# Retention plus gated layer on one core: three operand sums of the first seven-product tile moved together on VectorE, the others halved on GpSimd

## The chip, the cores and the metric

The kernel runs on one core of one Trainium2 chip. The time is device microseconds for one execution of the whole program; less is better. It is given as the median of five runs. A profile of one further execution shows where its time went. "n" counts token tiles, "x" the products of one tile, as in the code.

## The reference

Eight batches of 576 tokens, eight heads of 64: a retention layer (scores of q and k, times a decay per head and distance, lower triangle only, times v), whose output, laid out as 4608 tokens by 512, goes through a layer of width 2048:

```python
scores = scale * np.matmul(q, k.transpose(0, 1, 3, 2))
Dmat = np.where(rel >= 0, gamma[:, None, None] ** rel[None, :, :], 0.0)
x = np.matmul(scores * Dmat, v)        # to [4608, 512]
h = x @ w_in                           # [4608, 2048]
out = (h * np.cos(h)) @ w_out          # [4608, 512]
```

## The kernel before

**Groups and tiles.** Tokens are handled in 36 groups g of 128 for the retention part and in ten tiles n for the layer, of 512 tokens except n = 1 and 2 (256 each). Tile 3 (S7 in the code) is the first, and tile 9 the last, that uses the scheme described below. Everything is issued in an order written out by hand; each engine runs its own queue in that order, and waits are put in where data or buffers demand it.

**The retention part of a group.** `load` brings q, k and v from memory on SyncE's queue. `prep` scales q and k by the decays and casts v (L139, L140, L147, mostly on GpSimd). `transposes` turns the scaled q and k by a DMA transpose (L156). `scores` (L183) multiplies them into the two-bank tiles "a" and "b"; VectorE applies the mask (L192, tile `ret`). `states` (L242) makes the running state of a pair of groups in bank "b"; VectorE copies or adds it out (L263, L265), and ScalarE spreads it into blocks (L256). `attn_out` (L283, L296) uses state and `ret`, and ScalarE writes the result as x (L308). In tile 3, `unit7` does this for groups 12 to 15 between the products, in the order states, attention output, scores of the next pair. The second `scores` of a pair uses bank "b" and so must wait until L263 and L265 have read the states there.

**The layer.** `mm1` makes a block of h in PSUM (L323), ScalarE the cosine (L331), VectorE the product gT (L332). Tile 3 has eight such blocks i = 0 to 7.

**Seven products in place of eight.** From tile 3 on, gT and w_out are taken as two by two quarters, and the second matrix product is made by seven quarter products instead of eight (`mm2_seven`, `product`, L457). Their order is x = 3, 4, 5, 2, 1, 7, 6. Products 5, 2, 1, 7 and 6 need sums or differences of two quarters of gT first, which `g_sum` makes (L398). Its arguments are the tile, the product, and a range of the eight row blocks: 0 to 4 and 4 to 8 are the two halves, 0 to 8 is a whole sum. A half is a 128x1024 instruction, a whole 128x2048.

`g_sum` chooses the engine. In tile 3 products 5 and 1 and the second half of 6 are on VectorE, the rest on GpSimd; in the last tile 5 and 1 are on VectorE; in the others only 5. Behind each sum of product 5 a gate is set: the next sum that goes to GpSimd is made to wait for it ("port free" in the code). `sums_after` calls `g_sum` after the blocks of `mm1`; in tile 3, two more calls stand inside `mm2_seven`: whole sum 1 on VectorE ahead of the addition to u22, and the second half of 6 on VectorE ahead of the store of c12.

**The outputs of a tile.** Four quarters of the output are gathered in SBUF: c12, c21, u11 and u22. ScalarE copies, and VectorE adds or subtracts product after product (`add`, L477). Products 5, 2 and 6 accumulate onto PSUM tiles of earlier products, so they can begin only when these have been read: product 2 onto product 4's tile, which the first addition to u22 reads. Each `store` puts a DMA on SyncE's queue and calls `feed`, which issues the next preps on GpSimd, and transposes and loads on SyncE. In tile 3 `prep_next` handles group 16 between the sums on GpSimd; groups 17 to 21 follow from the stores.

Of the kernel before, what the change touches and what calls it, by code (L numbers as in the profile page):

```python
# [17 lines left out]
def kernel(  # L18
# [34 lines left out]
    widths = [512, 256, 256] + [512] * 7  # L53
# [3 lines left out]
    S7 = 3  # L57
# [42 lines left out]
    tiles = {}  # L100
# [253 lines left out]
    E2 = ET // 2  # L354
    N2 = DM // 2
    w_sum = {}

    def w_quarter(r, c):
        return w_out_sb[:, r * E2 : (r + 1) * E2, c * N2 : (c + 1) * N2]

    def w_sums(x, e0, e1):

        a, b, op_ = {
            3: ((0, 1), (1, 1), ALU.subtract),
            4: ((1, 0), (0, 0), ALU.subtract),
            1: ((0, 0), (1, 1), ALU.add),
            6: ((0, 0), (0, 1), ALU.add),
            7: ((1, 0), (1, 1), ALU.add),
        }[x]
        if x in (3, 4):  # L370
            w_sum[x] = w_quarter(*a)
        elif x not in w_sum:
            pool, tag = {1: (consts, "ws1"), 6: (first, "qs4"), 7: (first, "qT4")}[x]
            w_sum[x] = pool.tile([P, E2, N2], BF16, tag=tag, name=f"ws{x}")
        nc.vector.tensor_tensor(
            out=w_sum[x][:, e0:e1],
            in0=w_quarter(*a)[:, e0:e1],
            in1=w_quarter(*b)[:, e0:e1],
            op=op_,
        )  # L380

    def g_sum(n, x, e0, e1):

        gT = tiles["g", n]
        a, b, op_ = {
            5: ((0, 0), (0, 1), ALU.add),
            2: ((1, 0), (1, 1), ALU.add),
            1: ((0, 0), (1, 1), ALU.add),
            7: ((0, 1), (1, 1), ALU.subtract),
            6: ((1, 0), (0, 0), ALU.subtract),  # L390
        }[x]
        if ("gs", n, x) not in tiles:
            tiles["gs", n, x] = sump.tile([P, E2, 256], BF16, tag=f"gs{x}", name=f"gs{x}")
        i0, i1 = (
            gT[:, k * E2 + e0 : k * E2 + e1, r * 256 : (r + 1) * 256] for r, k in (a, b)
        )
        on_dve = {S7: x in (5, 1) or (x, e0) == (6, 4), len(widths) - 1: x in (5, 1)}.get(n, x == 5)
        i = (nc.vector if on_dve else nc.gpsimd).tensor_tensor(  # L398
            out=tiles["gs", n, x][:, e0:e1], in0=i0, in1=i1, op=op_
        )  # L400
        if x == 5:
            tiles["gate"] = i
        elif "gate" in tiles and not on_dve:
            tc.add_manual_dep(
                i.ins,
                tiles.pop("gate").ins.name,
                mybir.DependencyInfo(mybir.DependencyClass.Sync, mybir.DependencyReason.DATA),
                reason="port free",
            )

    def sums_after(n, i):

        if n == S7:
            if i < 4:
                w_sums(3 + i % 2, i // 2 * 4, i // 2 * 4 + 4)
            if i == 6:
                g_sum(n, 5, 0, 4)
                g_sum(n, 2, 0, 4)
            elif i == 7:
                g_sum(n, 5, 4, E2)  # L420
                g_sum(n, 2, 4, E2)
                g_sum(n, 7, 0, E2)
                prep_next()
                g_sum(n, 6, 0, 4)
        elif i in (3, 7):
            for x in (5, 2, 1, 7, 6):
                g_sum(n, x, i - 3, i + 1)

    last = len(widths) - 1

    def product(n, x):

# [34 lines left out]
    def mm2_seven(n, at):  # L467

        s0 = starts[n] // P
        pend = []  # L470

        def flush():
            while pend:
                pend.pop(0)()

        def add(out_, in0, in1, op_=ALU.add):
            pend.append(lambda: nc.vector.tensor_tensor(out=out_, in0=in0, in1=in1, op=op_))  # L477

        def new(tag):
            return op.tile([P, 2, N2], F32, tag=tag, name="ot")  # L480

        def store(t, r, c, s):
            r0 = starts[n] + r * 256
            nc.sync.dma_start(
                out[r0 : r0 + 256, c * N2 : (c + 1) * N2].rearrange("(j p) c -> p j c", p=P), t
            )
            feed(s)

        for x in (3, 4, 5, 2, 1, 7, 6):
            if x in at:  # L490
                at[x](flush)
            else:
                flush()
            parts = product(n, x)
            if x == 3:
                u22 = new("a")
                nc.scalar.copy(u22, tiles["all", 3])
            elif x == 4:
                if n == S7:
                    g_sum(n, 1, 0, E2)  # L500
                add(u22, tiles["all", 4], u22)
            elif x == 5:
                c12, u11 = new("c"), new("b")
                nc.scalar.copy(c12, tiles["all", 3])
                add(u11, u22, tiles["all", 3], ALU.subtract)
                if n == S7:
                    g_sum(n, 6, 4, E2)
                store(c12, 0, 1, s0)
            elif x == 2:
                c21 = new("d")  # L510
                nc.scalar.copy(c21, tiles["all", 4])
                add(u22, u22, tiles["all", 4], ALU.subtract)
                store(c21, 1, 0, s0 + 1)
            elif x == 1 and n < last:
                add(u11, tiles["all", 1], u11)
            elif x == 1:
                for (j, c0, c1), ps in zip(parts, tiles["o", 1]):
                    add(u11[:, j, c0:c1], ps, u11[:, j, c0:c1])
            elif x == 7:
                add(u11, tiles["all", 7], u11)  # L520
                flush()
                store(u11, 0, 0, s0 + 2)
            elif n < last:
                add(u22, tiles["all", 1], u22)
                flush()
                store(u22, 1, 1, s0 + 3)
            else:
                for (j, c0, c1), ps in zip(parts, tiles["o", 1]):
                    add(u22[:, j, c0:c1], ps, u22[:, j, c0:c1])
                    flush()  # L530
                    r0 = starts[n] + 256 + j * P
                    nc.sync.dma_start(out[r0 : r0 + P, N2 + c0 : N2 + c1], u22[:, j, c0:c1])
# [3 lines left out]
    def prep_next():  # L536
        nonlocal prepared
        prep(prepared)
        prepared += 1

    def feed(s):

        nonlocal loaded, prepared, transposed
        before = loaded
        n, r = divmod(s - starts[S7] // P, 4)
        if n >= 0:
            while prepared < min(NG, starts[S7] // P + 10 + 4 * n + ((0, 1, 2, 4) if n else (-1, 0, 1, 4))[r]):
                prep_next()
            while transposed < prepared:
                transposes(transposed)  # L550
                transposed += 1
            ahead = starts[S7] // P + 14 if n == 0 and r < 3 else prepared + LD
            while loaded < min(NG, prepared + LD, ahead):
                load(loaded)
                loaded += 1
            return
        while True:
            while prepared < min(loaded, 2 * s + 7, s + 11, starts[S7] // P + 8):
                prep(prepared)
                prepared += 1  # L560
                if transposed < N_PE_T:
                    transposed += 1

            if N_PE_T <= transposed < min(prepared, s + 11) and (
                transposed <= loaded - 2 or loaded == NG or (s > 3 and loaded == before)
            ):
                transposes(transposed)
                transposed += 1
            elif loaded < min(NG, 2 * s + 8, s + 13):
                load(loaded)  # L570
                loaded += 1
            else:
                break
# [144 lines left out]
    for n, w in enumerate(widths):  # L718
# [14 lines left out]
        for i, (et, c0, cw) in enumerate(blocks):  # L733

            inside = {
                (0, 0): {2: lambda: (attn_out([3], "n"), state(3))},
                (1, 0): {4: lambda: scores(5, "a")},
                (1, 1): {3: lambda: attn_out([5], "a", evac=nc.scalar.copy)},
            }.get((n, i), {})
            mm1(n, et, c0, cw, banks[i], inside)  # L740
            if (n, i) == (3, 1):
                late.pop()()
            if n >= S7:
                sums_after(n, i)
# [77 lines left out]
```

## Time and profile before

| | |
|---|---|
| time, median of 5 runs | 308.0 us (304.54 to 308.67) |
| profiled execution, its own time | 305.66 us |
| its span | 303.9 us |
| TensorE matmul busy | 293.0 us (96%) |
| VectorE busy | 208.7 us (69%) |
| GpSimd busy | 204.6 us (67%) |
| ScalarE busy | 145.7 us (48%) |
| mean granted TensorE clock | 0.986 |

All durations come from the profiled execution, whose times start at the span's start. PE is TensorE's matmul side, PEld its weight load, DVE VectorE, ACT ScalarE, POOL GpSimd, SPq the sequencer of SyncE. A line of a timeline gives start, length and instruction, with the count when instructions of a kind follow each other, and in brackets the idle time of the engine before it and what ended that. A record of the start of one instruction can lie up to 0.08 us before the end of the one before it. The second row of the page in the prediction is the granted clock in 40 slices of 7.6 us each, 9 meaning 90% or more of full clock.

### The profile page before, as it was taken

The page shows a single profiled execution, that of the slowest core. Times are in us where ns is not written, and L with a number is a line of the kernel's source. Part 1 is how long each engine was busy: PE and PEld are TensorE (multiplying, and loading weights), DVE is VectorE, ACT ScalarE, POOL GpSimd, SP SyncE. Part 2 cuts the span into 40 slices and gives each one's busy share as a digit, 9 for nine tenths or more (in the row PEclk, how much of TensorE's full clock was granted, in tenths as well). Part 3 has the DMA queues.
Part 4 walks back from the last instruction along what each step waited for, and adds up shares of the span by engine and source line. Part 5 has one row for each costly group of instructions (what it writes and reads, how often), then busy time and mean ns, then how long its engine had stood idle before and what let it go on. Part 6 is the DMA issues. An engine that isn't in the chain of part 4 may idle for free.

```text
span 303.9 us, 6662 instructions
## 1 busy us (share of the span) xinstructions
PE 293.0 (96%) x2761; PEld 200.8 (66%) x2761; DVE 208.7 (69%) x249; ACT 145.7 (48%) x187; POOL 204.6 (67%) x166
## 2 busy tenths in 40 slices
PE   8899999999999959999999999999999999999995
PEld 3478547757588747447754885488548854884584
DVE  5776646655699994487767774777478747835863
ACT  2656334415265341662356483647465646524620
POOL 2770078345347799859995999399949934970692
PEclk9999999999999987999999999999999999999999
DMA  8999999999999999999999975996760250022013
GB/s 210 211 210 207 205 226 201 202 251 212 192 204 215 202 247 200 251 224 190 208 232 202 244 160 113 206 229 151 152 159 2 71 138 2 0 71 69 2 35 104
DMA packets 154269, 50.23 MB, mean 165 GB/s; under 512 B 140800, under 2 KB 153216, under 8 KB 154240
## 3 DMA queue, kind: packets, MB, share of 16 engines
q1 hardware_dynamic: 150016, 45.63, 76.2%
q0 software_dynamic: 4224, 4.19, 8.3%
q8 instruction: 21, 0.34, 0.5%
q14 instruction: 8, 0.07, 0.1%
HBM read 36.70 MB, written 9.44 MB: 152 GB/s over the span
## 4 chain that ended last, share of the span: by engine, by line
PE 52%; DVE 3%; SPq 3%; POOL 2%; issue 1%; DMA 1%; POOLq 1%; ACT 0%; DVEq 0%
PE o L457 23%; PE h L323 22%; POOL gs L398 2%; PE ov L296 2%; PE sc L183 2%; PE ov L283 2%; DVE gs L398 1%; SPq L156 1%; DMA fv<-in_v_dram 1%; SPq L114 1%; PE st L242 1%; POOLq L817 1%; DVE ret L192 1%; DVE gT L332 0%; ACT cosh L331 0%
## 5 line engine op out<-in xcount | busy, mean ns | idle before, releaser
L398 POOL TENSOR_TENSOR gs<-gT 128x1024 bf16<-128x1024 bf16 (+1 forms) x50 | 110.4, 2241 | 42.0 <-DVE gs L398 36.9
L323 PE MATMUL h<-xT,w_in_sb 128*128 128x512 bf16 (+2 forms) x832 | 127.8, 314 | 0.3
L332 DVE TENSOR_TENSOR gT<-h,cosh 128x1024 bf16<-128x1024 f32 x72 | 87.9, 1223 | 43.6 <-ACT cosh L331 43.4
L331 ACT ACTIVATE cosh<-h,half_pi 128x1024 f32<-128x1024 f32 x72 | 80.2, 1114 | 63.7 <-PE h L323 62.8
L323 PEld LDWEIGHTS <-w_in_sb 128*128 128x128 bf16 x832 | 75.9, 98 | 49.4 <-issue 0.9
L457 PEld LDWEIGHTS <-gs 128*128 128x128 bf16 x576 | 55.0, 100 | 10.3 <-POOL gs L398 1.7
L139 POOL TENSOR_TENSOR qks<-fq,gq 128x512 bf16<-128x512 f32 x32 | 34.4, 1076 | 37.7 <-DMA fq<-in_q_dram 37.7
L140 POOL TENSOR_TENSOR qks<-fk,gk 128x512 bf16<-128x512 f32 x35 | 37.4, 1067 | 9.5 <-DMA fk<-in_k_dram 9.2
L457 PE MATMUL o<-ws,gs 128*128 128x256 bf16 (+1 forms) x352 | 40.9, 278 | 0.0
L192 DVE TENSOR_TENSOR ret<-sc,tri 128x1024 bf16<-128x1024 f32 x32 | 38.0, 1219 | 3.9 <-PE sc L183 3.8
L477 DVE TENSOR_TENSOR ot<-o,ot 128x512 f32<-128x512 f32 (+2 forms) x32 | 19.7, 621 | 17.7 <-PE o L457 17.6
L340 PE MATMUL o<-w_out_sb,gT 128*128 128x512 bf16 x128 | 30.1, 380 | 0.0
L308 ACT CAST xT<-ov 128x1024 bf16<-128x1024 f32 (+1 forms) x18 | 16.5, 918 | 28.2 <-PE ov L296 28.0
L457 PE MATMUL o<-w_out_sb,gs 128*128 128x256 bf16 x224 | 26.2, 273 | 0.9 <-POOL gs L398 0.8
L457 PE MATMUL o<-w_out_sb,gT 128*128 128x256 bf16 x224 | 25.6, 273 | 0.0
L457 PEld LDWEIGHTS <-gT 128*128 128x128 bf16 x224 | 21.8, 98 | 3.9
L340 PEld LDWEIGHTS <-gT 128*128 128x128 bf16 x128 | 11.8, 98 | 12.6
L398 DVE TENSOR_TENSOR gs<-gT 128x1024 bf16<-128x1024 bf16 (+1 forms) x18 | 17.8, 1000 | 0.4
L256 ACT CAST sb<-s 64x256 bf16<-64x256 f32 x40 | 16.1, 403 | 2.5 <-DVE s L263 2.0
L147 POOL CAST vb<-fv 128x512 bf16<-128x512 f32 x22 | 13.4, 609 | 3.0 <-DMA fv<-in_v_dram 2.4
L183 PE MATMUL sc<-qkT 64*128 64x128 bf16 x256 | 10.7, 220 | 3.4 <-DVE s L265 3.3
L183 PEld LDWEIGHTS <-qkT 64*128 64x128 bf16 x288 | 8.3, 95 | 8.6 <-DMA fq<-in_q_dram 3.4
(70 smaller groups left out, 171.2 us busy)
## 6 DMA issues: line engine op xcount, KB each, us to landing
out_dram<-ot SPq DMA_DIRECT2D x35, 256.0 KB, 3.4
fk<-in_k_dram SPq DMA_DIRECT2D x32, 256.0 KB, 5.1
fv<-in_v_dram SPq DMA_DIRECT2D x32, 256.0 KB, 5.2
fq<-in_q_dram SPq DMA_DIRECT2D x28, 256.0 KB, 4.5
w_in_sb<-in_moe_w_in_dram POOLq DMA_DIRECT2D x4, 512.0 KB, 8.7
w_out_sb<-in_moe_w_out_dram POOLq DMA_DIRECT2D x4, 512.0 KB, 15.9
fq<-in_q_dram SPq DMA_DIRECT2D x2, 512.0 KB, 4.3
fq<-in_q_dram SPq DMA_DIRECT2D x8, 128.0 KB, 4.6
```

The costliest lines, as they stand in the source:

```text
L139: nc.gpsimd.tensor_tensor(out=qks[:, 0], in0=fq, in1=tq, op=ALU.mult)
L140: (nc.vector if g == 3 else nc.gpsimd).tensor_tensor(out=qks[:, 1], in0=fk, in1=tk, op=ALU.mult)
L183: nc.tensor.matmul(ps[:, he, hg, :], lhsT=qkT[d0 : d0 + D, HG + hg, :], rhs=qT[d0 : d0 + D, hg, :], start=True, stop=True,)
L192: nc.vector.tensor_tensor(out=ret.rearrange("p a b i -> p (a b) i"), in0=ps.rearrange("p a b i -> p (a b) i"), in1=mask.unsqueeze(1).to_br ...
L308: evac(tiles["x", n][:, :, t0 : t0 + len(gs) * P].rearrange("p c (x i) -> p x c i", i=P), ps)
L323: nc.tensor.matmul(ps[:, j, :], lhsT=w_in_sb[:, dg, (et + j) * P : (et + j + 1) * P], rhs=xT[:, dg, c0 : c0 + w], start=(dg == 0), stop=(d ...
L331: nc.scalar.activation(cosh, ps, ACTF.Sin, bias=half_pi, scale=1.0)
L332: nc.vector.tensor_mul(gT[:, et : et + m, c0 : c0 + w], ps, cosh)
L340: nc.tensor.matmul(ps, lhsT=gT[:, et, tsi * P : (tsi + 1) * P], rhs=w_out_sb[:, et, :], start=(et == 0), stop=(et == ET - 1),)
L398: i = (nc.vector if on_dve else nc.gpsimd).tensor_tensor(out=tiles["gs", n, x][:, e0:e1], in0=i0, in1=i1, op=op_)
L457: nc.tensor.matmul(dst[i], lhsT=lhs[:, e, j * P : (j + 1) * P], rhs=rhs[:, e, c0:c1], start=(x in (3, 4, 1, 7) and e == 0 and (i == 0 or l ...
L477: pend.append(lambda: nc.vector.tensor_tensor(out=out_, in0=in0, in1=in1, op=op_))
```

## The change

In tile 3, the second half of sum 5, the second half of sum 2 and whole sum 1 follow each other on VectorE, right after the last block of `mm1`. Sum 7 goes to GpSimd as two halves: the first straight after the first half of sum 2, the second gated. Sum 6 goes to GpSimd as two halves after the prep of group 16. The two calls inside `mm2_seven` are gone. The gate is now set by every sum on VectorE, so that the next GpSimd sum in the program waits for the latest of them: the first half of 2 for the first half of 5, the second half of 7 for sum 1. In the last tile the order of the sums is 5, 1, 2, 7, 6 instead of 5, 2, 1, 7, 6, so that there sum 2 waits for sum 1. In tiles 4 to 8 nothing changes.

```diff
-        on_dve = {S7: x in (5, 1) or (x, e0) == (6, 4), len(widths) - 1: x in (5, 1)}.get(n, x == 5)
+        on_dve = x == 5 or (x == 1 and n in (S7, last)) or (n, x, e0) == (S7, 2, 4)
         i = (nc.vector if on_dve else nc.gpsimd).tensor_tensor(
             out=tiles["gs", n, x][:, e0:e1], in0=i0, in1=i1, op=op_
         )
-        if x == 5:
+        if on_dve:
             tiles["gate"] = i
-        elif "gate" in tiles and not on_dve:
+        elif "gate" in tiles:
             tc.add_manual_dep(
@@ sums_after
             if i == 6:
-                g_sum(n, 5, 0, 4)
-                g_sum(n, 2, 0, 4)
+                for x in (5, 2, 7):
+                    g_sum(n, x, 0, 4)
             elif i == 7:
-                g_sum(n, 5, 4, E2)
-                g_sum(n, 2, 4, E2)
-                g_sum(n, 7, 0, E2)
+                for x, e in ((5, 4), (2, 4), (1, 0), (7, 4)):
+                    g_sum(n, x, e, E2)
                 prep_next()
-                g_sum(n, 6, 0, 4)
+                for e in (0, 4):
+                    g_sum(n, 6, e, e + 4)
         elif i in (3, 7):
-            for x in (5, 2, 1, 7, 6):
+            for x in (5, 2, 1, 7, 6) if n < last else (5, 1, 2, 7, 6):
                 g_sum(n, x, i - 3, i + 1)
@@ mm2_seven
             elif x == 4:
-                if n == S7:
-                    g_sum(n, 1, 0, E2)
                 add(u22, tiles["all", 4], u22)
@@
                 add(u11, u22, tiles["all", 3], ALU.subtract)
-                if n == S7:
-                    g_sum(n, 6, 4, E2)
                 store(c12, 0, 1, s0)
```

More of the change, by code (lines that the diff above doesn't have):

```diff
@@ L356 @@
     w_sum = {}
+    last = len(widths) - 1
     def w_quarter(r, c):
@@ L416, in sums_after @@
             if i == 6:
-                g_sum(n, 5, 0, 4)
-                g_sum(n, 2, 0, 4)
+                for x in (5, 2, 7):
+                    g_sum(n, x, 0, 4)
             elif i == 7:
-                g_sum(n, 5, 4, E2)
-                g_sum(n, 2, 4, E2)
-                g_sum(n, 7, 0, E2)
+                for x, e in ((5, 4), (2, 4), (1, 0), (7, 4)):
+                    g_sum(n, x, e, E2)
                 prep_next()
-                g_sum(n, 6, 0, 4)
+                for e in (0, 4):
+                    g_sum(n, 6, e, e + 4)
         elif i in (3, 7):
-            for x in (5, 2, 1, 7, 6):
+            for x in (5, 2, 1, 7, 6) if n < last else (5, 1, 2, 7, 6):
                 g_sum(n, x, i - 3, i + 1)
-    last = len(widths) - 1
     def product(n, x):
```

## The prediction, made before the changed kernel was run

> **What bounds the kernel now.** I read the page first, then the waits, the chain of work that ended last, and the timelines of VectorE and GpSimd around the first seven-product tile (n = 3).
>
> ```profile
> PE 293.0 (96%) x2761; PEld 200.8 (66%) x2761; DVE 208.7 (69%) x249; ACT 145.7 (48%) x187; POOL 204.6 (67%) x166
> PEclk9999999999999987999999999999999999999999
> ...
> PE sc L183 <- DVE s L265: 3.3, 1, 3.3
> PE o L457 <- POOL gs L398: 0.8, 2, 0.6
> ```
>
> TensorE is busy 96% of the span: a microsecond counts only if TensorE stands still or runs slowly in it. One wait stands out: scores (L183) wait 3.3 us for VectorE's state add (L265), once. In the clock row only the 15th and 16th slices (106.4 to 121.6 us) are below 9. The chain shows both:
>
> ```profile
> 107.03 3.69 DVE gs L398
> 110.72 0.60 DVE ot L477
> 111.32 0.35 DVE s L263
> 111.66 0.02 issue
> 111.69 0.44 DVE s L265
> 112.12 0.14 issue
> 112.26 0.61 PE sc L183 x8
> 112.87 6.18 PE o L457 x32
> ...
> 146.53 3.60 PE o L457 x32
> ```
>
> The columns are start, length, what. A VectorE gT sum holds up the state add, it holds up the scores, and then 32 matmuls take 6.18 us, where the same 32 in the next tile take 3.60. Why the sum takes 3.7 us is in the two engines' timelines:
>
> ```profile
> 101.50 2.67 DVE L398 TENSOR_TENSOR gs<-gT 128x1024 bf16<-128x1024 bf16 x2
> 106.95 3.77 DVE L398 TENSOR_TENSOR gs<-gT 128x1024 bf16<-128x1024 bf16 x1
> ...
> 103.11 7.06 POOL L398 TENSOR_TENSOR gs<-gT 128x1024 bf16<-128x1024 bf16 x2 [0.63 <-DVE gs L398]
> 110.14 1.49 POOL L139 TENSOR_TENSOR qks<-fq,gq 128x512 bf16<-128x512 f32 x1
> ...
> L398 DVE TENSOR_TENSOR gs<-gT x2: 1212/1370/1529, 101.5 to 103.0; 128x1024 bf16<-128x1024 bf16 x1, 128x2048 bf16<-128x2048 bf16 x1
> ```
>
> I call a sum by its product and half (5b: product 5, second half). 6b on VectorE begins at 106.95, in the middle of GpSimd's whole sum 7 (about 106.13 to 110.17), and ends 0.55 us after it; alone such a half takes 0.68. GpSimd's next multiply takes 1.49 instead of 1.04. The last line gives 5b 1.53 us (GpSimd's 2a ran until 102.49) and whole sum 1 1.21.
>
> **What the Trainium skill says.** "SBUF — State Buffer", section Who interferes with whom: a VectorE instruction with two SBUF inputs and a GpSimd instruction that reads SBUF cannot run together; whoever issues first has the shared port for the whole instruction, the other fully blocks. The trace agrees: 0.68 became 3.77. "TensorE: Matmul & The Clock Gate", Part 1: the array drops to half clock by free-running windows of about 3.4 us with little activity. The trace agrees: after the stall the mean clock is 0.50 from 111.3 to 118.12 us and 1.00 on both sides. "GPSIMD Engine Reference", section 4.1 Engine selection: about 2x slower in two-input operations; here it is 2.12 us for a half against 0.68, three times.
>
> **The change part by part.** (1) 6b leaves VectorE's queue, where it stood ahead of the u11 subtraction, the state copy and the state add. (2) 2b goes from GpSimd to VectorE, whole sum 1 moves up behind it, ahead of the u22 add. (3) Whole sum 7 on GpSimd becomes 7a (no gate, straight after 2a) and 7b, which waits for sum 1; 6a and 6b follow the prep of group 16 on GpSimd. (4) In the last tile sum 1 goes ahead of 2, so 2's gate is sum 1, not sum 5. The order on TensorE and SyncE is the same.
>
> VectorE with the port in its hands: 5b ends at 103.03 as now; 2b costs 0.60 (0.68 less 0.08 of overlap between records), to 103.64; sum 1 1.13, to 104.77; the u22 add ends at 105.37 (104.77 now). Product 2 accumulates onto what that add reads, so it starts at about 105.43; by now's pace it could start at 105.04 (103.18 plus 16 matmuls of 0.116). It takes 1.86 us, to 107.29. Now it ends at 107.26, since it waits for 2b in its middle. Cost here: nothing. The two ret multiplies end at 107.63 instead of 107.03, and the state matmuls wait for them 0.5 us longer. Then, with 6b gone, u11, state copy and add follow at once, the add ends at 109.03 and the scores go on at 109.1, not 112.26: 3.2 us. The 32 matmuls take 3.60 instead of 6.18: 2.6 us. The next tile's first matmul comes at about 116.6 instead of 122.4: 5.8 us.
>
> What is late next is GpSimd:
>
> ```profile
> 127.66 0.61 POOL L147 CAST vb<-fv 128x512 bf16<-128x512 f32 x1
> 132.59 17.16 POOL L398 TENSOR_TENSOR gs<-gT 128x1024 bf16<-128x1024 bf16 x8 [4.31 <-DVE gs L398]
> 143.56 1.05 PE L457 MATMUL o<-w_out_sb,gs 128*128 128x256 bf16 x8 [0.58 <-POOL gs L398]
> ```
>
> The eight GpSimd sums of tile 4 start 10.2 us after that tile's first matmul, and GpSimd is idle for 4.31 us before them. Its preps end at 128.27 now and come no earlier after the change: 7a runs from about 104.64 to 106.76, 7b to 108.85, prep 16 (2.55) to 111.4, 6a and 6b (2.1 each) to 115.6, where now 6a ends at 115.26; five more groups of 2.55 give about 128.3. The loads of group 21 also land only near 127.6, by a SyncE queue that is full throughout and doesn't move. So the sums start at 128.3 instead of 132.6, their fifth (2b) ends 10.9 later, at 139.2, and TensorE, there at 137.2, waits 2 us. It passes this point 4.3 us earlier than now (143.5), not 5.8. In the later tiles GpSimd is idle for 3.5 to 12 us ahead of its sums and TensorE has no gap of 0.2 us, so the 4.3 stay.
>
> Last tile: 2a is held until 1a ends instead of 5a, some 0.2 us; 6a's end moves, so 5b, 1b and 2b move, and 2b is again held by 1b, another 0.2. Product 2 takes 2b with 0.07 us of waiting now, so about 0.45 us lands on the end. Bounds: 0.2 if only one shift counts, 0.9 if both double.
>
> Sum: 4.3 - 0.45 = 3.85 us off the profiled execution's 305.66 (span 303.9), giving 301.8. The median of the runs shown is 308.0, and they lie between 304.54 and 308.67. From the median it is 304.15, and I take 304.2.
>
> **The cost that the trace does not show** is who gets the port when 5b ends: 2b, next in VectorE's queue, or 7a, which by then has been waiting since 102.46. The trace shows five times that a waiting VectorE sum goes ahead of GpSimd's next one (at 138.65 us 5b took 0.78, and the GpSimd sum behind it was held 0.45); the reverse does not occur. Lower bound: nothing. Upper bound: 7a runs first, 2b ends at 105.57, sum 1 at 106.70, the u22 add at 107.30; product 2 starts at 107.35, TensorE having stood for 2.3 us; the next tile starts at 118.6. Because GpSimd bounds tile 4 anyway, TensorE passes the wait for 2b at about 139.7, and the gain is 3.8 - 0.45 = 3.35, or 304.65, as long as the clock stays up. I take the lower bound for the number and keep both.
>
> **Rivals.** *Half clock remains, less.* 7a gets the port, and the 2.3 us of standing fall into one window; 2.3 us of standing ahead of the change of clock did it in the trace (108.98 to 111.30). One window at half clock loses 1.7 us: the next tile starts at 120.3, gain 2.1 - 0.45 = 1.65, time 306.3. For it: by the skill, what issues first has the port, and 7a issued before 2b. Against: the window's phase, which isn't fixed to the kernel. The same may happen at the 2 us wait for 2b in tile 4.
>
> *Slower.* The same place and mechanism, but the clock stays at half for three windows (10.2 us) from 107.9 on, as the ret multiplies and state steps behind it keep TensorE sparse: 5.1 us lost, the next tile starts at 123.7, 1.3 later than now, and with the last tile's 0.45 the time is 309.8. It decides from about 6 us at half clock on; the trace has 6.8 after a longer stall. Against it: at half clock TensorE is fuller, not emptier.
>
> *More than forecast.* The median falls to the low end of what the runs show, the sum taken off 304.6: 300.8.
>
> **How the numbers follow.** Forecast (stall and half clock gone, either order at the port) 0.60, its own range 303.3 to 305; half clock remains 0.24; slower than now 0.08; the low level 0.08. The range 300.8 to 307.8 leaves out the slow case and the tails. A measurement of this kernel can hardly tell less than 1% (3.1 us) from no change, and the forecast lies only 0.7 us beyond that: faster 0.52, same 0.40, slower 0.08.
>
> **What would show it right or wrong.** Right: the wait of L183 for L265 is gone, no VectorE sum of tile 3 but 5b is over 0.8 us, the 32 matmuls take 3.6 us, the next tile's matmuls start near 117 to 119, the GpSimd sums of tile 4 start near 128.3 and TensorE waits about 2 us for 2b. The forecast's order is wrong if 2b takes over 2 us behind 7a. The prediction is wrong if the clock row still shows two low slices, if the preps end after 129, or if the last tile's end slips by over 1 us.

## The result, and the profile after

The changed kernel takes 303.71 us in the median of 40 runs (302.5 to 308.99), the kernel before 305.98 in 75 runs (302.94 to 312.08; the five shown at first are among them). The ratio is taken from the runs that lie within 1.5% of the fastest of their kernel, so it is not that of these two medians: 0.9951, with a 95% interval from 0.9934 to 0.9968; a second set of runs gave 0.9932 (0.9904 to 0.9960). So the change is faster, by 0.5 to 0.7%, some 1.5 to 2 us; the forecast was 1.2% (3.85 us).

The profiled execution of the changed kernel took 308.25 us, with a span of 306.5: it reached tile 3 5.6 us late, held up first by a wait of 2.42 us for a transposed group, which the change doesn't touch. Times are therefore counted from here on from the start of the first VectorE sum of tile 3, 5a: at 99.60 us before, at 105.18 after. To the end of the last matmul it is 200.62 us before and 197.67 after, 2.95 less.

First the waits of the changed kernel (who waited for whom, total, times, longest):

```profile
PE o L456 <- DVE ot L476: 2.2, 1, 2.2
PE o L456 <- POOL gs L399: 1.5, 2, 0.9
```

The wait of the scores for L265 is gone. In its place product 2 waits 2.2 us for the first addition to u22. The timelines of VectorE, GpSimd and TensorE, each in its own lines, show why:

```profile
107.08 5.19 DVE L399 TENSOR_TENSOR gs<-gT 128x1024 bf16<-128x1024 bf16 x3
112.20 0.68 DVE L476 TENSOR_TENSOR ot<-o,ot 128x512 f32<-128x512 f32 x1
...
105.94 4.64 POOL L399 TENSOR_TENSOR gs<-gT 128x1024 bf16<-128x1024 bf16 x2 [4.83 <-DVE gs L399]
112.35 2.13 POOL L399 TENSOR_TENSOR gs<-gT 128x1024 bf16<-128x1024 bf16 x1 [1.76 <-DVE gs L399]
...
108.76 1.92 PE L456 MATMUL o<-w_out_sb,gs 128*128 128x256 bf16 x16
112.93 1.91 PE L456 MATMUL o<-w_out_sb,gs 128*128 128x256 bf16 x16 [2.25 <-DVE ot L476]
117.13 3.67 PE L456 MATMUL o<-ws,gs 128*128 128x256 bf16 x32
```

VectorE's three sums take 5.19 us; singly they are 1.53 (5b), 2.60 (2b) and 1.21 (sum 1). GpSimd's 2a and 7a end at 110.59. So 2b, which takes 0.68 alone, ran after 7a: the three did not run without a break. Behind sum 1 comes the u22 add, and behind that product 2. The later part of the tile is as forecast: no stall at the scores, the 32 matmuls in 3.67 us.

What follows in tile 4 and in the last tile, in the chain of work that ended last:

```profile
133.49 1.06 DVE gs L399
...
143.48 2.13 POOL gs L399
145.61 0.05 issue
145.66 1.05 PE o L456 x8
...
296.53 6.34 PE o L456 x72
302.87 0.02 issue
```

The first matmul of tile 4 comes 18.8 us after 5a instead of 22.6, 3.8 earlier. The fifth GpSimd sum of tile 4 ends 40.42 after 5a instead of 43.91: only 3.5 are left. The last 72 matmuls start 0.53 us later, counted from the end of the wait for that sum (296.53 - 145.66 = 150.87, before 293.90 - 143.56 = 150.34). TensorE leaves that wait 3.48 us earlier than before (40.48 us after 5a instead of 43.96), and 3.48 - 0.53 = 2.95, the whole difference. The first line is tile 4's own 5a, which takes 1.06 us where before it took 0.69.

### The profile page after: what moved, and what is told of

Same layout as the page of the kernel before. It is cut to its first block, busy times and chain, and to the rows that moved or that the text cites. A ratio compares the mean times of both kernels' runs of the same rounds, so it can differ in the third digit from the quotient of the medians.

```text
span 306.5 us, 6663 instructions
## 1 busy us (share of the span) xinstructions
PE 292.5 (95%) x2761; PEld 200.2 (65%) x2761; DVE 209.7 (68%) x249; ACT 145.5 (47%) x187; POOL 202.8 (66%) x167
## 4 chain that ended last, share of the span: by engine, by line
PE 52%; POOL 4%; DVE 3%; issue 2%; POOLq 1%; ACT 1%; DVEq 0%
PE h L323 23%; PE o L456 22%; POOL gs L399 4%; PE ov L296 2%; PE ov L283 2%; PE sc L183 2%; PE st L242 1%; DVE gT L332 1%; DVE gs L399 1%; DVE ret L192 1%; ACT cosh L331 1%; POOLq L812 1%; DVE ot L476 0%; DVEq L812 0%; POOLq L399 0%
## 5 line engine op out<-in xcount | busy, mean ns | idle before, releaser
L399 POOL TENSOR_TENSOR gs<-gT 128x1024 bf16<-128x1024 bf16 x51 | 109.4, 2181 | 43.7 <-DVE gs L399 43.7
L456 PEld LDWEIGHTS <-gs 128*128 128x128 bf16 x576 | 53.7, 98 | 11.8 <-issue 2.4
L139 POOL TENSOR_TENSOR qks<-fq,gq 128x512 bf16<-128x512 f32 x32 | 33.5, 1046 | 39.2 <-DMA fq<-in_q_dram 37.5
L456 PE MATMUL o<-ws,gs 128*128 128x256 bf16 (+1 forms) x352 | 38.3, 268 | 0.0
L340 PE MATMUL o<-w_out_sb,gT 128*128 128x512 bf16 x128 | 30.9, 387 | 0.0
L350 ACT COPY ot<-o 128x512 f32<-128x512 f32 x8 | 4.7, 588 | 20.4 <-PE o L340 20.4
L183 PEld LDWEIGHTS <-qkT 64*128 64x128 bf16 x288 | 8.2, 94 | 7.9 <-DMA qkT<-qks 2.6
```

Source lines behind the costliest of these rows:

```text
L139: nc.gpsimd.tensor_tensor(out=qks[:, 0], in0=fq, in1=tq, op=ALU.mult)
L340: nc.tensor.matmul(ps, lhsT=gT[:, et, tsi * P : (tsi + 1) * P], rhs=w_out_sb[:, et, :], start=(et == 0), stop=(et == ET - 1),)
L399: i = (nc.vector if on_dve else nc.gpsimd).tensor_tensor(out=tiles["gs", n, x][:, e0:e1], in0=i0, in1=i1, op=op_)
L456: nc.tensor.matmul(dst[i], lhsT=lhs[:, e, j * P : (j + 1) * P], rhs=rhs[:, e, c0:c1], start=(x in (3, 4, 1, 7) and e == 0 and (i == 0 or l ...
```

## The experiments

Two groups of four kernels, each beside runs of the kernel before on the same chip. The medians scatter by chance more than the edits differ. Much of what varies lies ahead of tile 3: in the ten profiles 5a starts anywhere from 99.60 to 105.18 us, while the changed kernel, profiled twice, takes the same from there to the end within 0.02 us. So the verdicts rest on the traces, in us after the start of 5a, with the ratio to the kernel before beside them. "Filled" means that matmuls of zeros stand in the gap, and the number is what is left of it.

| kernel | stall at product 2 or at the scores | tile 4 starts | first GpSimd sum of tile 4 | fifth ends | last tile, matmuls | last matmul ends | ratio (interval) |
|---|---|---|---|---|---|---|---|
| before | 3.29 (scores) | 22.63 | 32.98 | 43.91 | 26.48 | 200.62 | 1 |
| changed | 2.25 (product 2) | 18.80 | 29.50 | 40.42 | 27.02 | 197.67 | 0.9951 (0.9934 to 0.9968) |
| e8 changed, again | 2.26 (product 2) | 18.81 | 29.50 | 40.44 | 27.01 | 197.69 | 0.9932 (0.9904 to 0.9960) |
| e1 clock kept | 0.16 (filled) | 19.83 | 30.18 | 41.11 | 26.49 | 197.83 | 0.9878 (0.9810 to 0.9947) |
| e2 six moved | 0.25 | 18.26 | 30.81 | 41.72 | 26.48 | 198.43 | 0.9888 (0.9829 to 0.9947) |
| e3 seven held | 0.33 | 17.13 | 29.68 | 40.59 | 27.01 | 197.84 | 0.9872 (0.9798 to 0.9945) |
| e4 tail back | 2.26 (product 2) | 19.85 | 30.20 | 41.13 | 26.47 | 197.84 | 0.9858 (0.9793 to 0.9924) |
| e5 held and tail | 0.33 | 17.12 | 29.66 | 40.57 | 26.49 | 197.29 | 0.9930 (0.9894 to 0.9967) |
| e6 casts on ScalarE | 0.33 | 17.14 | 28.59 | 39.51 | 26.48 | 196.22 | 0.9919 (0.9886 to 0.9951) |
| e7 gap filled | 0.31 (filled) | 18.80 | 29.51 | 40.42 | 27.01 | 197.67 | 0.9928 (0.9900 to 0.9955) |

e1 to e4 ran on one chip, with a median of 309.05 for the kernel before; e5 to e8 on another, with 305.65. Ratios of the two groups are not to be set against each other.

**e1: the clock kept up, the stall left in.** In `unit7`, tile 3, first pair, of the kernel before:

```diff
-            scores2(g + 2)
+            scores(g + 2, "a", idle=14)
+            scores(g + 3, "b")
```

> The kernel before, with 14 matmuls of zeros (0.216 us each, 3.0 us) ahead of the scores of group 14, so that TensorE is busy while it would stand; every wait stays. Theory (the half clock after the stall is a good part of what there is to gain, but the kernel before does not lose it in the same measure in every run): the 32 matmuls of products 1 and 7 take 3.6 us instead of 6.2, tile 4 starts some 2.6 us earlier than in the profile of before, the mean clock is 1.00 in nearly every run, and the ratio of the times is 0.993 to 0.997, since the clock of before varies from run to run. Rival (the clock costs as much in every run as in the profile): ratio 0.991 or less. Rival (the clock costs nothing in typical runs): ratio 1.000.

The stretch was 2.79 us shorter, with the same VectorE sum of 3.76 us in it and the 32 matmuls at full clock:

```profile
110.76 3.76 DVE L398 TENSOR_TENSOR gs<-gT 128x1024 bf16<-128x1024 bf16 x1
...
112.60 2.97 PE L174 MATMUL sc<-zeros 128*128 128x512 bf16 x13 [0.16 <-issue]
116.39 3.67 PE L457 MATMUL o<-ws,gs 128*128 128x256 bf16 x32
```

So the half clock alone is worth nearly as much as the whole difference between the profile of before and that of the changed kernel (2.79 of 2.95); the 3.3 us stall itself is worth only 0.54 more (e5, with the same last tile and no stall of over 0.4 us ahead of tile 4, takes 197.29). The mean clock was 0.998 or 1.000 in six of seven runs. How much before loses in a typical run can be estimated from the clock of its 59 runs in the second group. One stretch of 3.4 us at half clock, called a window here, goes with a mean clock of 0.994 (the profile of e4), two with 0.986 (that of before): in 34 the mean clock is 0.992 to 0.994 (lowest time 304.28), in 23 it is 0.981 to 0.989 (lowest 305.49), in two 1.000 (lowest 304.28). The profiled execution, with 0.986 and 6.8 us at half clock, belongs to the dearer kind, by about 1.2 us. What the first window costs, two runs are too few to say. The ratio, 0.988, came out lower than either the theory or the rival "no cost" had it, but its interval holds both 0.991 and 0.993, so it doesn't choose between the theory and the first rival. That the cost varies from run to run, as the theory has it, is shown by the clocks. In the first group 9 of the 11 runs of before had a clock of 0.989 or less, but that does not explain why all four ratios of that group are low: 8 of the 11 took over 307 us, while two with a clock of 0.986 took 305.42 and 305.58. What held up the others is not in a trace.

**e2: 6b moved and nothing else.** From the kernel before:

```diff
-        on_dve = {S7: x in (5, 1) or (x, e0) == (6, 4), len(widths) - 1: x in (5, 1)}.get(n, x == 5)
+        on_dve = {S7: x in (5, 1), len(widths) - 1: x in (5, 1)}.get(n, x == 5)
                 g_sum(n, 6, 0, 4)
+                g_sum(n, 6, 4, E2)
-                if n == S7:
-                    g_sum(n, 6, 4, E2)
```

> The kernel before, with the second half of sum 6 of tile 3 on GpSimd behind its first half, and nothing else. Theory (6b on VectorE behind GpSimd's whole sum 7 is the stall, and it alone): no VectorE sum above 1.6 us, the 3.3 us wait of the scores for the state add is gone, the 32 matmuls take 3.6 us; GpSimd's preps end about 1.7 us later (near 130) and bound tile 4, so TensorE passes the wait for its 2b some 2.6 us earlier than in the profile of before, and the ratio is about that of the changed kernel, 0.993 to 0.997. Rival (the stall goes only if 2b and sum 1 move as well): the wait of 3 us stays and the ratio is 1.000.

As expected, the stall and the half clock go with 6b alone: tile 4 starts at 18.26, sooner than in the changed kernel. The 2b and sum 1 moves aren't needed for that. But GpSimd has 2.1 us more to do. TensorE waits 0.60 and 1.03 us for the two halves of sum 6 at the end of tile 3; the first GpSimd sum of tile 4 starts only at 30.81, since 5a on VectorE took 2.89 us (none above 1.6 was expected), and TensorE waits there too:

```profile
134.51 1.89 PE L323 MATMUL h<-xT,w_in_sb 128*128 128x512 bf16 x8 [1.34 <-DVE gT L332]
144.44 1.05 PE L458 MATMUL o<-w_out_sb,gs 128*128 128x256 bf16 x8 [1.27 <-POOL gs L398]
```

The stretch is 2.2 us shorter than before, where 2.6 was expected, and 0.76 longer than in the changed kernel, though the last tile is 0.5 cheaper. The changed kernel has one half, 2b, less on GpSimd ahead of tile 4, and its preps end at 28.81 after 5a, here at 30.11.

**e3: 7a held too.** From the changed kernel:

```diff
-                for x in (5, 2, 7):
+                for x in (5, 2):
                     g_sum(n, x, 0, 4)
-                for x, e in ((5, 4), (2, 4), (1, 0), (7, 4)):
-                    g_sum(n, x, e, E2)
+                for x, e in ((5, 4), (2, 4), (1, 0), (7, 0), (7, 4)):
+                    g_sum(n, x, e, 4 if (x, e) == (7, 0) else E2)
```

> The changed kernel, with the first half of sum 7 behind the gate too (7a after sum 1 on GpSimd). Theory (at the end of 5b the waiting 7a takes the port ahead of 2b, and 2b's 1.9 us of waiting is TensorE's 2.25 us stall ahead of product 2): 2b takes 0.7 us instead of 2.6, the stall ahead of product 2 falls to about 0.4, tile 4 starts 2.0 us earlier, but GpSimd's preps end no earlier and TensorE then waits 2 to 3 us for 2b of tile 4; the time falls only 0.3 to 0.6 us against the changed kernel. Rival (the stall ahead of product 2 comes from the order of VectorE's queue, sum 1 ahead of the u22 add): 2.25 us stay. Rival (tile 4 is not bounded by GpSimd): 2 us faster than the changed kernel.

The three VectorE sums now take 3.27 us, 2b 0.68 of them, and product 2 waits 0.33:

```profile
104.13 3.27 DVE L399 TENSOR_TENSOR gs<-gT 128x1024 bf16<-128x1024 bf16 x3
...
108.06 1.91 PE L456 MATMUL o<-w_out_sb,gs 128*128 128x256 bf16 x16 [0.33 <-DVE ot L476]
```

Tile 4 starts 1.67 us earlier than in the changed kernel. This settles that 7a caused the 2.25 us. And the stretch to the end is 197.84, no shorter at all: the fifth sum of tile 4 ends at 40.59 against 40.42. The 1.67 us went into waits of TensorE in tile 4: a new one of 1.34 for gT, behind 5a, which takes 2.89 us here, and 1.27 for 2b instead of 0.93. The "0.3 to 0.6 less" was wrong: there was nothing.

**e4: the last tile as before.** From the changed kernel:

```diff
-        if on_dve:
+        if on_dve and (n < last or x == 5):
-        elif "gate" in tiles:
+        elif "gate" in tiles and not on_dve:
-            for x in (5, 2, 1, 7, 6) if n < last else (5, 1, 2, 7, 6):
+            for x in (5, 2, 1, 7, 6):
```

> The changed kernel, with the order and the gate of the last tile as before (5, 2, 1, 7, 6; sum 2 waits for sum 5 alone). Theory (the last tile's gate costs about 0.5 us on the end): from the first matmul of the last tile to the end of the span 0.5 us less than in the changed kernel, and the time 0.4 to 0.6 us lower. Rival (it is hidden): no difference.

From the last tile's first matmul to the last one 26.47 us instead of 27.02: 0.55, as expected. The stretch as a whole came out 0.17 longer than in the changed kernel, because here a half clock followed the 2.26 us at product 2. In these lines, stretches of the execution, the granted clock is the column after POOL's, the third from the end:

```profile
107.70:108.60 0.90, 0.88 (x9) 0.78 (x9) 0.90 (x1) 0.00 (x0) 0.90 (x1) 1.00 1.02 224
108.60:112.00 3.40, 3.40 (x40) 2.44 (x39) 2.82 (x6) 0.59 (x1) 3.40 (x5) 0.50 1.14 254
112.00:114.00 2.00, 2.00 (x42) 1.70 (x37) 1.69 (x2) 1.46 (x3) 2.00 (x2) 0.99 1.16 262
```

One window of 3.4 us puts tile 4 1.05 us later than in the changed kernel's profile, which has no half clock here, and the fifth sum 0.71 later.

**e7: the gap at product 2 filled.** From the changed kernel:

```diff
+            if n == S7 and x == 2:
+                warm(psum.tile([P, 512], F32, tag="m", name="idle"), 9)
             parts = product(n, x)
```

> The changed kernel with 9 matmuls of zeros (0.216 us each, 1.9 us) ahead of product 2 of tile 3, where TensorE stands for 2.25 us; every wait stays. Theory (in some runs the 2.25 us fall into one window and the clock is halved for 3.4 us, about 0.7 to 1 us lost): the mean clock is 1.00 in all runs where nothing else held TensorE up, against 0.994 in about half the runs of the changed kernel, and the time is 0.3 to 0.6 us lower in the mean. Rival (the clock falls for another reason): 0.994 as often as in the changed kernel.

In 12 of 13 runs the mean clock is 0.998 or more, against 13 of 22 in e8 on the same chip. But a mean clock of 0.994 doesn't say where in the execution the window lies. The profiled execution of the changed kernel, 308.25 us with 0.994, has it ahead of tile 3, behind the wait for the transposed group, and full clock around product 2 and after it:

```profile
83.88:87.30 3.42, 3.42 (x20) 1.70 (x20) 1.69 (x2) 0.58 (x1) 1.08 (x2) 0.66 1.38 164
112.20:124.00 11.80, 10.72 (x161) 9.11 (x161) 9.22 (x14) 4.74 (x9) 11.65 (x10) 1.00 1.12 194
```

The profiles of e8 (307.35 us) and e5 (307.71) have it there too. So the eight runs of the first 40 with 0.993 or 0.994 and over 307 us tell nothing of product 2. Of the runs that the ratios are taken from, 12 of 32 had 0.994 then, 6 of 19 in e8, and none of 12 in e7. So in these the half clock does come from the 2.25 us. An estimate of its price is the distance of the lowest times in e8: 302.68 at 0.998 and more, 303.34 at 0.994, that is 0.66 us; in the first 40 runs it is 0.74 (302.50 and 303.24). Both are near the 0.71 of e4's fifth sum. The means of the same runs, 303.19 in e7 and 303.70 in e8, lie 0.5 apart, as expected, though the two ratios cannot be told apart.

**e8, e5, e6: what bounds tile 4.** e8 is the changed kernel again:

> The changed kernel itself, as the yardstick of the three others on this chip. From the start of the first VectorE sum of tile 3 to the last matmul: 197.7 us at full clock, as in its first profile, and about 0.7 more where a half-clock window falls on product 2.

It repeats its stretch to 0.02 us. e5 is e3 and e4 together:

> The changed kernel with sum 7 held behind sum 1 and the last tile as before. Theory (tile 4 is bounded by GpSimd; holding 7a back moves the wait from product 2 of tile 3 to tile 4, and the last tile's gate costs 0.5): the stall ahead of product 2 is 0.4, the fifth GpSimd sum of tile 4 ends about 40.6 us after the first VectorE sum of tile 3, as with 7a in front, and from that sum to the last matmul it is 197.3 us, 0.4 to 0.5 less than in the changed kernel; the clock is 1.00 there in every run. Rival (the two changes add up, 2.0 + 0.5): 195.2 us.

197.29 against 197.3. It is 0.38 less than in the changed kernel: the tail gives its 0.5, and the held 7a nothing, since the fifth sum ends 0.15 later. e6 takes 1.2 us of work off GpSimd on top of e5:

```diff
-            copy_v = nc.scalar.copy if g > starts[S7] // P + 17 else nc.gpsimd.tensor_copy
+            copy_v = nc.scalar.copy if g > starts[S7] // P + 17 or g in (17, 18) else nc.gpsimd.tensor_copy
```

> The kernel with sum 7 held and the last tile as before, and the v casts of groups 17 and 18 on ScalarE instead of GpSimd (1.2 us less on GpSimd between the sums of tiles 3 and 4). Theory (GpSimd's preps bound tile 4): the preps end 1.2 us earlier, the fifth sum of tile 4 too, near 39.4 us after the first VectorE sum of tile 3, and from that sum to the last matmul it is about 196.2 us. Rival (the landing of the loads of groups 20 and 21 bounds the preps): the casts make room, the preps wait for the loads instead, and the gain is under 0.4 us. Rival (something on TensorE's side bounds tile 4): no gain.

The fifth sum ends at 39.51 and the stretch is 196.22, both near what the theory said (39.4 and 196.2); but the way there was in part another. First e5's VectorE and GpSimd ahead of tile 4's sums, then e6's:

```profile
131.36 1.04 POOL L139 TENSOR_TENSOR qks<-fq,gq 128x512 bf16<-128x512 f32 x1
131.62 2.88 DVE L399 TENSOR_TENSOR gs<-gT 128x1024 bf16<-128x1024 bf16 x1
132.36 1.04 POOL L140 TENSOR_TENSOR qks<-fk,gk 128x512 bf16<-128x512 f32 x1
133.34 0.61 POOL L147 CAST vb<-fv 128x512 bf16<-128x512 f32 x1
134.64 2.13 POOL L399 TENSOR_TENSOR gs<-gT 128x1024 bf16<-128x1024 bf16 x1 [0.69 <-DVE gs L399]
```

```profile
126.80 1.51 DVE L399 TENSOR_TENSOR gs<-gT 128x1024 bf16<-128x1024 bf16 x1
...
126.71 1.04 POOL L140 TENSOR_TENSOR qks<-fk,gk 128x512 bf16<-128x512 f32 x1
127.85 0.92 POOL L147 CAST vb<-fv 128x512 bf16<-128x512 f32 x1
128.74 4.21 POOL L399 TENSOR_TENSOR gs<-gT 128x1024 bf16<-128x1024 bf16 x2
```

In e5 tile 4's 5a, on VectorE, waits through three prep instructions of GpSimd until the last is over, and GpSimd's first sum waits for 5a through the gate. In e6 the preps end only 0.33 us earlier (28.63 after 5a of tile 3 instead of 28.96), where the theory had 1.2. The three of group 21 now have gaps of about 0.1 us before them, and the landing times in the trace show why, as the rival said: the loads of group 21 land at 125.44, 126.64 and 127.73 us, each 0.07 to 0.13 ahead of the start of its prep (in e5 they land 3.5 to 3.8 us ahead). 5a ends in e6 before the preps do. Its 1.51 us fit a turn in the gap ahead of the last prep, which takes 0.92 us in place of 0.61. GpSimd then goes straight on to its sums, 1.07 us earlier.

e6 is the best of the versions run: 1.45 us less than the changed kernel from 5a to the end. Its lowest time, 301.29, compares with 302.68 for e8 and 304.28 for before on the same chip. By ratio to before, 0.9919 against 0.9932, the intervals overlap. In 7 of the 20 runs that its ratio is taken from, the mean clock is 0.994 or less, at 302.89 us and more. TensorE's wait for 2b of tile 4, 1.55 us in e6, may bring this on; no trace shows such a run.

## Why the prediction was right or wrong

- **Direction and range: right.** 303.71 lies in 300.8 to 307.8, close to 304.2. But the relative change is about half of the forecast; the agreement in microseconds is in part luck. It is owed to the starting point, 308.0 from five runs, where 75 runs have a median of 305.98; the same 3.85 us off that would have been 302.1.
- **The stall and its cause: right.** 6b behind GpSimd's whole sum was the 3.3 us wait (e2 takes it away alone), and the half clock behind it was a cost of its own (e1).
- **"Lower bound: nothing" at the port: wrong.** The step that failed is the order when 5b ends. I took 2b to go first; 7a goes first, in all four profiles with that order (the changed kernel twice, e4, e7), and 2b takes 2.60 us instead of 0.68. What I kept as the upper bound came out nearly to the number: stall 2.25 (2.3 worked out), tile 4 3.8 us earlier (3.8). The five cases that I had counted for it were of the opposite kind, a VectorE sum waiting behind a GpSimd sum, and told nothing about a GpSimd sum waiting behind a VectorE sum; I took the lower bound for the number all the same. By the section Who interferes with whom of the Trainium skill's "SBUF — State Buffer", whoever issues first has the port; 7a had issued ahead of 2b, so the page pointed to the answer that the runs show.
- **"What is late next is GpSimd": right, and it decides the size.** The preps of tile 3's groups end 28.8 us after 5a (28.7 predicted), the first sum of tile 4 starts at 29.5 (28.7 predicted), and 3.5 of 3.8 us survive. e3 shows how hard the bound is: 1.67 us gained ahead of it gave nothing. I had missed the 0.7 us between preps and sums: 5a itself waits for the preps.
- **The last tile: right.** 0.45 predicted, 0.55 measured (e4), and paid in full.
- **The mis-sized term: the half clock.** I took 2.6 us off the profiled execution as if every run paid it. In the second group the lowest time of the 34 runs with one window is 1.2 us below that of the 23 with more. Taking 1.2 from 2.95 leaves 1.75. Of the 32 runs of the changed kernel that its ratio is taken from, 12 pay about 0.7 for their own window, 0.3 on average. That leaves 1.5, an estimate, near the 1.5 that a ratio of 0.9951 means; the second set of runs, 0.9932, means 2.1.
- **Rivals.** "Half clock remains, less" describes 12 of these 32 runs, at about 0.7 us in place of 1.7: in e4 the window puts the start of tile 4 back by 1.05 us, and GpSimd's bound in tile 4 hides part of that. "Slower" did not come about: no profile shows a second window in a row at product 2.
- **The signs named beforehand.** The wait of L183 is gone, the 32 matmuls take 3.67 us, the preps end in time and the last tile slips by 0.5, as said. Two did not hold. TensorE waits 0.93 us for 2b of tile 4, not 2, because it arrives later. And "no VectorE sum of tile 3 but 5b is over 0.8 us" could not have held: whole sum 1 takes 1.21 by itself, as the prediction has it elsewhere.

## What to carry to other kernels

Where two engines share a port, an order in one engine's queue is no promise of a run without a break: an ungated instruction of the other engine that is already waiting can go in between, as 7a did here, so everything that is to stay out must be held, not only the last piece. A microsecond gained ahead of the next bound is lost again in waiting for it (1.67 us in e3): look for what that bound waits for, here GpSimd's preps and their gate, before a second stall is taken away. And a clock that drops after a stall differs from run to run: take its cost from the clocks of many runs, not from one profile.

## What the runs showed of the hardware

A waiting VectorE sum gets in between two GpSimd sums: in tiles 4 to 8 of before, 5b takes 0.7 to 1.1 us, and the GpSimd sum behind it 2.57 or 2.58 instead of 2.12. A waiting GpSimd sum gets in between two VectorE sums: 7a ahead of 2b, which takes 2.60 us instead of 0.68. But it does not get in between GpSimd's prep instructions where these follow each other without a gap: in e2, e3 and e5 the VectorE sum took 2.88 or 2.89 us, until the last prep was over, while in e6, with gaps of about 0.1 us, it took 1.51. There the rule of the page "SBUF — State Buffer", whoever issues first, does not describe what happens: by the records the sum begins 0.7 us ahead of the second of the preps that it waits for. Why sums and preps differ in this stays open; their records overlap alike by about 0.04 us.
